# Gated mix of two cached attention branches, one token: the last values in the values' tile, and branch A's output weights in two halves around them

## Chip, cores, metric

The kernel runs on one core of one Trainium2 chip. The metric is device time in microseconds of one execution, the median of several runs.

## What is computed

Two attention branches A and B, each for a batch of 2, one query token, 32 heads of 128 and 4096 cached tokens, all in float32; their outputs are mixed by a gate from the input:

```python
def branch(x, k_cache, v_cache, wq, wo):          # x [2,1,512], caches [2,32,4096,128]
    q = (x @ wq).reshape(B, 1, 32, 128).transpose(0, 2, 1, 3)
    p = softmax(einsum("bhqd,bhkd->bhqk", q, k_cache) * 128 ** -0.5)
    o = einsum("bhqk,bhkd->bhqd", p, v_cache)
    return o.transpose(0, 2, 1, 3).reshape(B, 1, 4096) @ wo     # wo [4096, 512]

x = A_x                                            # both branches take A's input
g = sigmoid((x * gate_w).sum(-1, keepdims=True))
out = g * branch(x, A...) + (1 - g) * branch(x, B...)
```

Nearly all of the data are the four caches, 128 MB each; the four weight matrices have 8 MB each.

## The kernel before

The work is cut into 32 units of 4 heads of one batch entry of one branch. A unit's keys are 8 MB, its values too, and each fills one tile of 128 partitions by 128 tokens by 128 numbers: a partition holds 128 tokens of one head. There are three such tiles, `kt[0]` and `kt[1]` for keys of even and odd units and `vt` for values, and no room for a fourth.

For a unit VectorE (DVE) multiplies the keys by the query (L392), sums over the head's 128 numbers (L395) and finds the maximum (L400 to L402); ScalarE (ACT) takes the exponentials (L367) into `padded` (`pr` in the profile), a tile of weights with empty places that keep heads apart; TensorE (PE) multiplies weights and values in 32 matmuls that add up in PSUM tile `vp` (L371). ACT then clears the used places of `padded` (L430). Units go in pairs, the two batch entries of the same heads. After the second of a pair, `vp` holds both and is picked apart into `vs` (L451, L416).

Each engine runs a loop of its own over pairs (TensorE over units), and semaphores with counts tie them: `k_free[i]` is raised when DVE is done with a keys' tile, `v_free` when ACT has cleared the weights after a unit's products, `summed` when TensorE is done with a unit, `weights` when ACT is, `v_landed` when values have landed. The loads stand on SP's queue, in program order: keys of unit u + 1, values of unit u, each behind a wait for its tile (`load_k`, `load_v`). A wait on SP holds up all requests behind it; the transfers run one behind the other.

The last unit is different. Its values don't go to `vt` but to `kt[0]`, which the last even unit's keys have left, so they can be requested before the product of unit 30 is done. TensorE's loop runs over 31 units (`products(NU - 1)`), and `last_products` multiplies unit 31's values straight from `kt[0]`. Branch A's output weights (`wo["A"]`, one transfer of 8 MB) then go into `vt`, and branch B's into `kt[1]`, in seven transfers that get smaller.

The tail then is: products of unit 31; `vs` of the last pair (L542, L544); per-head sums of `vs` over partitions (L548, `heads`) and of the exponentials (L560, `bank`); division by sums times gate (L575) into `on`; the output product, `project_out` for A's 32 rows and B's first 24 (L466, into `most`), and `project_last` for B's last 8 (L481), which gathers in four PSUM tiles with a folded copy of `most` (L582, L586). The tail's small tiles are cut out of a keys' tile that has been read (`Scratch(kt[0])`).

Of the kernel before, what the change touches and what calls it, by code (L numbers as in the profile page):

```python
# [8 lines left out]
AF = mybir.ActivationFunctionType  # L9
# [4 lines left out]
B = 2  # L14
H = 32
SK = 4096
DH = 128
D = 512
# [3 lines left out]
NS = SK // PH  # L22
# [3 lines left out]
NVC = NS // VC  # L26
QT = 32
STRIPS = P // QT
OR = H * DH // P
# [18 lines left out]
class Streams:  # L48
# [32 lines left out]
    def put(self, e, make, reads=(), writes=(), gives=None):  # L81

        self.before(e, reads, writes)
        i = make(self.engines[e])
        if gives is not None:
            i.then_inc(gives, 1)
            return None
        self.ticks[e] += 1
        i.then_inc(self.sems[e], 1)
        point = self.sems[e], self.ticks[e]  # L90
        self.after(point, reads, writes)
        return point
# [18 lines left out]
class Round:  # L111
# [12 lines left out]
    def do(self, make, after=0, gives=None):  # L124
        self.wait(after)
        i = make(self.x)
        if gives is None:
            self.n += 1
        i.then_inc(gives or self.sem, 1)
        return self.n  # L130
# [13 lines left out]
def tile_gated_decode(ctx: ExitStack, tc: tile.TileContext, ins: dict, out: bass.AP):  # L144
    nc = tc.nc
# [5 lines left out]
    NU = len(units)  # L151
# [5 lines left out]
    slot = small.tile([P, VC], F32, name="slot")  # L157
# [9 lines left out]
    vs = small.tile([P, NP, DH], F32, name="vs")  # L167
# [4 lines left out]
    kt = [big.tile([P, NS, DH], F32, name=f"kt{i}") for i in range(2)]  # L172
    vt = big.tile([P, NS, DH], F32, name="vt")
# [3 lines left out]
    vp = ps.tile([P, VC * DH], F32, name="vp")  # L177
# [4 lines left out]
    with tc.tile_critical(no_gpsimd_drain=True):  # L182
        S = Streams(nc, tc)
        put, take = S.put, S.take
        R = Region
        r_kt = [R(), R()]
        r_vt = R()
        r_pad, r_lp, r_sc, r_across, r_qsel = (R() for _ in range(5))
# [6 lines left out]
        v_landed, k_landed = sem("v_landed"), [sem(f"k_landed{i}") for i in range(2)]  # L195
        v_free, k_free = sem("v_free"), [sem(f"k_free{i}") for i in range(2)]
        weights, summed = sem("weights"), sem("summed")
# [5 lines left out]
        def tokens(cache, u):  # L203
            n, g, b = units[u]
            rows = ins[n + cache].rearrange("b h s d -> (b h s) d")
            r0 = (b * H + g * G) * SK
            return rows[r0:r0 + G * SK].rearrange("(p r) d -> p r d", p=P)
# [3 lines left out]
        def load_parts(item, t, src, slots, *cuts):  # L211
            parts[item] = [S.dma("sp", t[:, i:j], src[:, i:j], slot=s) for s, i, j in zip(slots, cuts, cuts[1:])]

        def arrived(e, item, *which):
            p = parts[item]
            S.wait(e, [p[k] for k in which] if which else p)
# [16 lines left out]
        def load_v(u):  # L233
            if u == 0:
                S.before("sp", [], [r_vt])
            elif u < NU - 1:
                nc.sync.wait_ge(v_free, u)
            if u < NU - 1:
                nc.sync.dma_start(vt, tokens("_v_cache", u)).then_inc(v_landed, 16)
            else:  # L240
                nc.sync.wait_ge(k_free[0], NU // 2)
                load_parts(("v", u), kt[0], tokens("_v_cache", u), "g", 0, NS)

        def load_wo(n):
            t = wo[n]
            src = ins[n + "_wo"].rearrange("(p r) e -> p r e", p=P)
            if n == "A":
                nc.sync.wait_ge(v_free, NU - 1)
                load_parts(("wo", n), t, src, "f", 0, OR)
                return  # L250
            nc.sync.wait_ge(k_free[1], NU // 2)
            load_parts(("wo", n), t, src, "abchi", 0, OR // 2, EARLY, OR - 4, OR - 2, OR - 1)
            parts["wo", n] += [S.dma("sp", t[:, OR - 1, h], src[:, OR - 1, h], slot=s) for s, h in zip("jk", HALVES)]

        wo = {n: t.rearrange("p r d -> p (r d)").rearrange("p (r e) -> p r e", e=D) for n, t in (("A", vt), ("B", kt[1]))}


        class Scratch:
# [3 lines left out]
            def take(self, n):  # L262
                self.at += -(-n // 128) * 128
                return self.t[:, self.at - -(-n // 128) * 128:][:, :n]

        start = Scratch(kt[1]).take
        rows, ident, xg, w, every, e, more = (start(n) for n in (D, P, B * KC, B, P, B, STRIPS * B * G))
        r_rows, r_gatew, r_ident, r_xg, r_w, r_every, r_e, r_more = (R() for _ in range(8))

        def vput(e, make, reads=(), writes=(), **kw):  # L270
# [6 lines left out]
                                     slot="y"))  # L277
# [84 lines left out]
        def exps(u, b, pair, do):  # L362

            s, m = sc[u % 2], nm[u % 2]
            for j, h in enumerate(QUARTERS):
                at = bass.ds(pair * (B * G) + (b * G + j), 1)
                do(lambda x: x.activation(padded[h, :, b, j * VC:(j + 1) * VC], s[h].rearrange("p (c a) -> p c a", a=VC),  # L367
                                          AF.Exp, bias=m[h], accum_out=lp[h, at]), weights if j == G - 1 else None)

        def chunk(x, c, t):  # L370
            return x.matmul(vp[c % STRIPS * QT:(c % STRIPS + 1) * QT], padded[:, c].rearrange("p b m -> p (b m)"),  # L371
                            t[:, c * VC:(c + 1) * VC].rearrange("p a d -> p (a d)"), start=False, stop=False,
                            skip_group_check=True)

        def products(n):
            with nc.Fori(0, n, engines=[mybir.EngineType.PE]):
                take("pe", weights)
                take("pe", v_landed, 16)
                for c in range(NVC):
                    i = chunk(nc.tensor, c, vt)  # L380
                i.then_inc(summed, 1)

        def last_products():
            S.wait("pe", r_pad.writers)
            arrived("pe", ("v", NU - 1))
            for c in range(NVC - 1):
                chunk(nc.tensor, c, kt[0])
            r_kt[0].readers = [put("pe", lambda x: chunk(x, NVC - 1, kt[0]), [], [r_vp])]


        def whole_scores(o, after):
            at = D_.do(lambda x: x.tensor_tensor(kt[o], kt[o], q[:, None, :].to_broadcast([P, NS, DH]), op=ALU.mult), after)  # L392
# [15 lines left out]
        def dve_second(nxt):  # L408
            take("dve", k_landed[1], 16)
            maxima_of(1, whole_scores(1, 0))  # L410
            return next_queries(nxt, 0) if nxt else 0
# [17 lines left out]
        def clear_padded(b):  # L429
            return A_.do(lambda x: x.activation(padded[:, :, b], nil[:, :, None].to_broadcast([P, NVC, G * VC]), AF.Copy))  # L430

        def act_exps(u, b, pair):
            take("act", maxima)
            exps(u, b, pair, lambda make, gives: A_.do(make, 0, gives))

        def act_second(pair, last=False):
            take("act", summed)
            at = clear_padded(0)
            A_.tell(v_free, at)
            A_.tell(spare, at)  # L440
            if not last:
                act_exps(1, 1, pair)
                return
            A_.close()
            take("act", maxima)
            exps(1, 1, pair, lambda make, gives: put("act", make, [], [R()]))
            r_lp.writers = r_pad.writers = [(S.sems["act"], S.ticks["act"])]

        def act_first(pair, nxt):
            take("act", summed)  # L450
# [7 lines left out]


        def project_out(k, n, *rows_):  # L460
            bounds = (0,) if n == "A" else (0, OR // 2)
            for r in range(*rows_):
                if r in bounds:
                    arrived("pe", ("wo", n), bounds.index(r))
                s = r % STRIPS
                put("pe", lambda x: x.matmul(most[s * QT:s * QT + B], on[:, k, r], wo[n][:, r],  # L466
                                             start=n == "A" and r < STRIPS, stop=n == "B" and r >= EARLY - STRIPS),
                    [r_on], [r_most])
# [40 lines left out]
        for u in range(2, NU):  # L509
            load_k(u)  # L510
            load_v(u - 1)
        load_v(NU - 1)
        load_wo("A")
        load_wo("B")

        exps(0, 0, 0, lambda make, gives: put("act", make, [r_nm[0], r_sc, r_pad, r_lp, r_nil], [], gives))
# [6 lines left out]
        with nc.Fori(0, NP - 1, engines=[mybir.EngineType.Activation]) as i:  # L523
            act_second(i)
            act_first(i, i + 1)
        products(NU - 1)
        dve_second(None)
        act_second(NP - 1, last=True)
        D_.close()

        last_products()
        end = Scratch(kt[0]).take
        sums, turned, laid, outs, kept = end(2 * B * P), end(D), end(P), end(P), end(D)
        drawn, onp = end(D), end(2 * OR * B)
        on = onp.rearrange("p (n r b) -> p n r b", n=2, b=B)
        totals = [end(D // 2)[:B] for _ in HALVES]
        r_sums, r_drawn, r_turned, r_laid, r_outs, r_kept = R(), R(), R(), [R() for _ in range(2 * B)], R(), R()
        for r in (r_sums, r_drawn, r_turned, r_outs, r_kept, r_on, *r_laid):
            r.readers = list(r_kt[0].readers)

        last = NP - 1
        put("act", lambda x: x.activation(vs[:, last], vp[:, :DH], AF.Copy, scale=slot[:, :1]), [r_vp], [r_vs])  # L542
        for a in range(1, VC):
            put("dve", lambda x: x.scalar_tensor_tensor(vs[:, last], vp[:, a * DH:(a + 1) * DH], slot[:, a:a + 1], vs[:, last],  # L544
                                                        op0=ALU.mult, op1=ALU.add), [r_vs, r_vp], [r_vs])
# [20 lines left out]
        for n in range(2):  # L566
            for b in range(B):
                c = n * B + b
# [24 lines left out]
        for h, e in enumerate(("sp", "act")):  # L593
            copied, r_total = sem(f"copied{h}"), R()
            for i in range(2):
                _, a, t, _ = next(strips(2 * h + i))
# [28 lines left out]
```

## Time and profile before

| | |
|---|---|
| median of 3 runs | 1324.14 us (1324.11 to 1324.51) |
| profiled execution: span from first to last instruction | 1322.3 us |
| what lies around the span (1324.14 - 1322.3; the profiled execution has no time of its own listed) | 1.8 us |
| moved by DMA | 570.51 MB, 431 GB/s over the span |
| busy: DVE / PE / ACT | 1165.3 / 331.7 / 100.7 us |
| granted TensorE clock, mean | 0.631 |

Times are in microseconds from the span's start unless marked ns. In the profile a line number belongs to the kernel above; a helper's line stands for all that it issues (L106 for the requests of `S.dma`, L97 for the waits of `take`, L134 for the counts of `tell`). `SPq` is SP's queue of requests; `x64` at a matmul counts passes, of which a float32 matmul has two. Requests count as not busy, so the DMA row and the landings show what the transfers do.

### The profile page before, as it was taken

The numbers are of one execution on the slowest core, as the hardware profiler recorded it, in microseconds if no ns is written. First come the engines' busy times: TensorE is split into PE (matmuls) and PEld (weight loads), VectorE is DVE, ScalarE is ACT, GpSimd is POOL, SyncE is SP. The second block draws the span as 40 slices with busy tenths as digits, with TensorE's granted clock in tenths as the row PEclk, the third lists the DMA queues.
The fourth block names the chain that finished last, engine by engine and source line by source line (L and its number), as shares of the span: only waits on it lengthen the run. The fifth ranks groups of instructions, "written<-read, shape, count | busy, mean of one in ns | idle before, by whom it ended". The sixth has DMA issues, their size and how long they took to land. (4 is left out here: it accounts for less than half of the span.)

```text
span 1322.3 us, 6216 instructions
## 1 busy us (share of the span) xinstructions
PE 331.7 (25%) x2382; PEld 90.3 (7%) x2382; DVE 1165.3 (88%) x316; ACT 100.7 (8%) x328; POOL 0.7 (0%) x6
## 2 busy tenths in 40 slices
PE   3112222211222221122222122222212322311256
PEld 0000000000000000000000000000000000000011
DVE  1978999999999999999999999999999999999961
ACT  0000100001010000101000010100001010000100
POOL 0000000000000000000000000000000000000000
PEclk9566666556666655666665666666556666555678
DMA  9999999999999999999999999999999999999998
GB/s 404 453 412 443 442 416 442 442 416 442 442 418 442 440 436 424 442 440 418 442 440 418 442 442 416 442 442 424 436 442 436 422 442 440 418 442 442 417 442 352
DMA packets 10820, 570.51 MB, mean 431 GB/s; under 512 B 1207, under 2 KB 1467, under 8 KB 1726
## 3 DMA queue, kind: packets, MB, share of 16 engines
q1 hardware_dynamic: 10804, 570.43, 99.6%
q8 instruction: 3, 0.05, 0.0%
q14 instruction: 3, 0.02, 0.0%
q10 hardware_dynamic: 10, 0.01, 0.0%
HBM read 570.43 MB, written 0.00 MB: 431 GB/s over the span
## 5 line engine op out<-in xcount | busy, mean ns | idle before, releaser
L392 DVE TENSOR_TENSOR kt<-kt,q 128x16384 f32<-128x16384 f32 x31 | 534.0, 17226 | 71.3 <-DVEq L97 71.3
L395 DVE TENSOR_REDUCE sc<-kt 128x128 f32<-128x16384 f32 x31 | 533.8, 17220 | 1.1
L371 PE MATMUL vp<-vt,pr 128*32 128x512 f32 x1984 | 283.1, 734 | 915.5 <-PEq L97 915.5
L371 PEld LDWEIGHTS vp<-vt,pr 128*32 128x32 f32 x1984 | 77.9, 132 | 1120.7 <-issue 1120.7
L367 ACT ACTIVATE pr<-sc,nm 32x128 f32<-32x128 f32 x128 | 50.9, 398 | 108.1 <-ACTq L97 102.8
L430 ACT ACTIVATE pr<-nil 128x512 f32<-128x512 f32 x31 | 19.3, 623 | 456.8 <-ACTq L97 456.8
L451 ACT ACTIVATE vs<-vp,slot 128x128 f32 x15 | 5.5, 368 | 448.1 <-ACTq L97 448.1
L337 PE MATMUL qa<-vt,cols 128*2 128x512 f32 x128 | 18.4, 739 | 39.9 <-PEq L97 39.9
L367 ACT ACTIVATION_READ_ACCUMULATOR pr<-sc,nm (+1 forms) x128 | 23.5, 184 | 0.0
L416 DVE SCALAR_TENSOR_TENSOR vs<-vp,slot,vs 128x128 f32 x45 | 15.8, 351 | 8.6 <-DVEq L97 7.6
L599 DVE COPY kt<-qa 2x128 f32<-2x128 f32 x1 | 0.3, 278 | 23.8 <-PE qa L481 23.8
L352 DVE STREAM_TRANSPOSE vt<-vt 128x1024 f32<-128x1024 f32 x2 | 2.4, 1224 | 17.1 <-ACT vt L348 17.1
L498 DVE TENSOR_REDUCE sc<-kt 128x64 f32<-128x8192 f32 x2 | 17.4, 8686 | 0.1
L496 DVE TENSOR_TENSOR kt<-kt,q 128x8192 f32<-128x8192 f32 x2 | 17.4, 8688 | 0.0
L455 ACT ACTIVATE vp<-nil 128x512 f32<-128x512 f32 x15 | 9.0, 600 | 99.2 <-ACTq L97 99.2
L544 DVE SCALAR_TENSOR_TENSOR vs<-vp,slot,vs 128x128 f32<-128x128 f32 x3 | 1.1, 351 | 12.9 <-ACT vs L542 12.8
L371 PE MATMUL vp<-kt,pr 128*32 128x512 f32 x64 | 9.0, 724 | 10.9 <-DMA kt<-in_B_v_cache_dram 10.9
L466 PE MATMUL most<-vt,kt 128*2 128x512 f32 x64 | 9.6, 765 | 6.5 <-DMA vt<-in_A_wo_dram 6.5
L400 DVE TENSOR_REDUCE rm<-sc 128x1 f32<-128x128 f32 x31 | 8.7, 281 | 2.3
L406 DVE STREAM_TRANSPOSE q<-qsel 128x128 f32<-128x128 f32 x30 | 9.3, 311 | 1.0
L289 DVE COPY cols<-bank 128x8 f32<-128x8 f32 x1 | 0.2, 167 | 10.0 <-PE bank L287 10.0
L401 DVE STREAM_TRANSPOSE across<-rm 128x32 f32<-128x32 f32 x31 | 6.6, 212 | 1.1
(73 smaller groups left out, 60.4 us busy)
## 6 DMA issues: line engine op xcount, KB each, us to landing
kt<-in_A_k_cache_dram SPq DMA_DIRECT2D x2, 4096.0 KB, 35.6
kt<-in_B_wo_dram SPq DMA_DIRECT2D x1, 4096.0 KB, 33.1
kt<-in_B_wo_dram SPq DMA_DIRECT2D x1, 2048.0 KB, 37.6
kt<-in_B_wo_dram SPq DMA_DIRECT2D x1, 1024.0 KB, 39.5
kt<-in_B_wo_dram SPq DMA_DIRECT2D x1, 512.0 KB, 40.3
vt<-in_A_v_cache_dram SPq DMA_DIRECT2D x16, 28.5
kt<-in_B_k_cache_dram SPq DMA_DIRECT2D x16, 42.6
kt<-in_B_wo_dram SPq DMA_DIRECT2D x1, 256.0 KB, 40.4
```

Of the source, the lines that this page charges most:

```text
L337: last = nc.tensor.matmul(t[h * QT:h * QT + B], cols[:, c], blocks[:, c, i, h], start=c == 0, stop=c == KC - 1)
L367: do(lambda x: x.activation(padded[h, :, b, j * VC:(j + 1) * VC], s[h].rearrange("p (c a) -> p c a", a=VC), AF.Exp, bias=m[h], accum_out=l ...
L371: return x.matmul(vp[c % STRIPS * QT:(c % STRIPS + 1) * QT], padded[:, c].rearrange("p b m -> p (b m)"), t[:, c * VC:(c + 1) * VC].rearran ...
L392: at = D_.do(lambda x: x.tensor_tensor(kt[o], kt[o], q[:, None, :].to_broadcast([P, NS, DH]), op=ALU.mult), after)
L395: at = D_.do(lambda x: x.tensor_reduce(sc[o], kt[o], axis=AX.X, op=ALU.add), at)
L406: return D_.do(lambda x: x.transpose(q, qsel[:, 0].to_broadcast([P, DH // QT, QT])), at)
L416: at = D_.do(lambda x: x.scalar_tensor_tensor(vs[:, g], vp[:, a * DH:(a + 1) * DH], slot[:, a:a + 1], vs[:, g], op0=ALU.mult, op1=ALU.add) ...
L430: return A_.do(lambda x: x.activation(padded[:, :, b], nil[:, :, None].to_broadcast([P, NVC, G * VC]), AF.Copy))
L455: A_.do(lambda x: x.activation(vp, nil.to_broadcast([P, VC * DH]), AF.Copy))
L466: put("pe", lambda x: x.matmul(most[s * QT:s * QT + B], on[:, k, r], wo[n][:, r], start=n == "A" and r < STRIPS, stop=n == "B" and r >= EA ...
L496: put("dve", lambda x: x.tensor_tensor(t, t, q[:, None, :].to_broadcast([P, NS // 2, DH]), op=ALU.mult), [r_q], [r])
L498: put("dve", lambda x: x.tensor_reduce(sc[0][:, h * NS // 2:(h + 1) * NS // 2], t, axis=AX.X, op=ALU.add), [r], [R()])
```

## The change

Unit 31's values go into `vt` like all others, behind a wait for `v_free`, and TensorE's loop runs over all 32 units; `last_products` is gone. Branch A's output weights go into `kt[0]` in two transfers of 4 MB, the first requested ahead of unit 31's values, the second behind them. The tail's small tiles are cut out of `vt`. The wait for the last unit's products is the loop's count `summed`.

```diff
         def load_v(u):
             if u == 0:
                 S.before("sp", [], [r_vt])
-            elif u < NU - 1:
+            else:
                 nc.sync.wait_ge(v_free, u)
-            if u < NU - 1:
-                nc.sync.dma_start(vt, tokens("_v_cache", u)).then_inc(v_landed, 16)
-            else:
-                nc.sync.wait_ge(k_free[0], NU // 2)
-                load_parts(("v", u), kt[0], tokens("_v_cache", u), "g", 0, NS)
+            nc.sync.dma_start(vt, tokens("_v_cache", u)).then_inc(v_landed, 16)
 
-        def load_wo(n):
+        def load_wo(n, h=0):
...
             if n == "A":
-                nc.sync.wait_ge(v_free, NU - 1)
-                load_parts(("wo", n), t, src, "f", 0, OR)
+                if h == 0:
+                    nc.sync.wait_ge(k_free[0], NU // 2)
+                load_parts(("wo", n, h), t, src, "fg"[h], h * OR // 2, (h + 1) * OR // 2)
                 return
...
-        wo = {... (("A", vt), ("B", kt[1]))}
+        wo = {... (("A", kt[0]), ("B", kt[1]))}
...
-        def last_products():
-            S.wait("pe", r_pad.writers)
-            arrived("pe", ("v", NU - 1))
-            for c in range(NVC - 1):
-                chunk(nc.tensor, c, kt[0])
-            r_kt[0].readers = [put("pe", lambda x: chunk(x, NVC - 1, kt[0]), [], [r_vp])]
...
         def project_out(k, n, *rows_):
-            bounds = (0,) if n == "A" else (0, OR // 2)
             for r in range(*rows_):
-                if r in bounds:
-                    arrived("pe", ("wo", n), bounds.index(r))
+                if r % (OR // 2) == 0:
+                    h = r // (OR // 2)
+                    arrived("pe", *((("wo", n, h), 0) if n == "A" else (("wo", n), h)))
...
+        load_wo("A", 0)
         load_v(NU - 1)
-        load_wo("A")
+        load_wo("A", 1)
         load_wo("B")
...
-        products(NU - 1)
+        products(NU)
...
-        last_products()
-        end = Scratch(kt[0]).take
+        end = Scratch(vt).take
...
-        put("act", lambda x: x.activation(vs[:, last], vp[:, :DH], AF.Copy, scale=slot[:, :1]), [r_vp], [r_vs])
+        take("act", summed)
+        r_lp.writers = [put("act", lambda x: x.activation(vs[:, last], vp[:, :DH], AF.Copy, scale=slot[:, :1]), [r_vp], [r_vs])]
```

On SP's queue, at the end of the loads, the requests stand in another order. In these rows `kt_85` is `kt[0]` and `kt_86` is `kt[1]`, and 128x16384 are 8 MB:

```order
 L231 DMA kt_86<-in_B_k_cache_dram 128x16384
-L239 DMA vt<-in_B_v_cache_dram 128x16384
-L106 DMA kt_85<-in_B_v_cache_dram 128x16384
-L106 DMA vt<-in_A_wo_dram 128x16384
+L238 DMA vt<-in_B_v_cache_dram 128x16384
+L106 DMA kt_85<-in_A_wo_dram 128x8192
+L238 DMA vt<-in_B_v_cache_dram 128x16384
+L106 DMA kt_85<-in_A_wo_dram 128x8192
 L106 DMA kt_86<-in_B_wo_dram 128x8192
 L106 DMA kt_86<-in_B_wo_dram 128x4096
```

The last values have moved one place back, behind half of A's weights, and the other half has come behind them.

On TensorE, from the last unit's products to the output rows of branch B, before (with the semaphores that each row waits for; `landed_g` is the last values, `landed_f` A's weights, `landed_a` B's first part):

```order
L371 MATMUL vp<-kt_85,pr 32x512 [waits landed_g,done_act]
L371 MATMUL vp<-kt_85,pr 32x512 x30
L371 MATMUL vp<-kt_85,pr 32x512 [waits done_dve]
L548 MATMUL heads<-vs,pick 32x512 [waits done_dve]
L548 MATMUL heads<-vs,pick 32x512 x3
L560 MATMUL bank<-ones,kt_85 128x1 [waits done_dve]
L560 MATMUL bank<-ones,kt_85 128x1 x3
L466 MATMUL most<-vt,kt_85 2x512 [waits done_dve,landed_f]
L466 MATMUL most<-vt,kt_85 2x512 x31
L466 MATMUL most<-kt_86,kt_85 2x512 [waits landed_a]
```

And the same place after, from the loop that now runs for all 32 units (`landed_f` and `landed_g` are the two halves of A's weights):

```order
L368 MATMUL vp<-vt,pr 32x512 x31
L373 REGISTER_ALU
L373 COMPARE_AND_BRANCH
L535 MATMUL heads<-vs,pick 32x512 [waits done_dve]
L535 MATMUL heads<-vs,pick 32x512 x3
L547 MATMUL bank<-ones,vt 128x1 [waits done_act,done_dve]
L547 MATMUL bank<-ones,vt 128x1 x3
L455 MATMUL most<-kt_85,vt 2x512 [waits done_dve,landed_f]
L455 MATMUL most<-kt_85,vt 2x512 x15
L455 MATMUL most<-kt_85,vt 2x512 [waits landed_g]
L455 MATMUL most<-kt_85,vt 2x512 x15
L455 MATMUL most<-kt_86,vt 2x512 [waits landed_a]
```

The separate 32 products are gone into the loop, and A's output rows wait in two places, at row 0 and at row 16, and no longer once for all.

More of the change, by code (lines that the diff above doesn't have):

```diff
@@ L253, in load_wo @@
             parts["wo", n] += [S.dma("sp", t[:, OR - 1, h], src[:, OR - 1, h], slot=s) for s, h in zip("jk", HALVES)]
-        wo = {n: t.rearrange("p r d -> p (r d)").rearrange("p (r e) -> p r e", e=D) for n, t in (("A", vt), ("B", kt[1]))}
+        wo = {n: t.rearrange("p r d -> p (r d)").rearrange("p (r e) -> p r e", e=D) for n, t in (("A", kt[0]), ("B", kt[1]))}
         class Scratch:
@@ L445, in act_second @@
             take("act", maxima)
-            exps(1, 1, pair, lambda make, gives: put("act", make, [], [R()]))
-            r_lp.writers = r_pad.writers = [(S.sems["act"], S.ticks["act"])]
+            exps(1, 1, pair, lambda make, gives: put("act", make, [], [R()], gives=gives))
         def act_first(pair, nxt):
@@ L537, in tile_gated_decode @@
         r_sums, r_drawn, r_turned, r_laid, r_outs, r_kept = R(), R(), R(), [R() for _ in range(2 * B)], R(), R()
-        for r in (r_sums, r_drawn, r_turned, r_outs, r_kept, r_on, *r_laid):
-            r.readers = list(r_kt[0].readers)
         last = NP - 1
-        put("act", lambda x: x.activation(vs[:, last], vp[:, :DH], AF.Copy, scale=slot[:, :1]), [r_vp], [r_vs])
+        take("act", summed)
+        r_lp.writers = [put("act", lambda x: x.activation(vs[:, last], vp[:, :DH], AF.Copy, scale=slot[:, :1]), [r_vp], [r_vs])]
         for a in range(1, VC):
```

## The prediction, made before the change was run

> **What bounds the kernel now.** I read the page first: shares, queue row, chain.
>
> ```profile
> span 1322.3 us, 6216 instructions
> PE 331.7 (25%) x2382; PEld 90.3 (7%) x2382; DVE 1165.3 (88%) x316; ACT 100.7 (8%) x328; POOL 0.7 (0%) x6
> DMA  9999999999999999999999999999999999999998
> q1 hardware_dynamic: 10804, 570.43, 99.6%
> DMA 3%; DVE 3%; PE 0%; SPq 0%; issue 0%; ACT 0%; DVEq 0%
> DMA kt<-in_B_wo_dram 3%; DVE kt L392 1%; DVE sc L395 1%; PE qa L481 0%; SPq L106 0%; PE vp L481 0%; ACT kt L598 0%; PE qa L586 0%; PE bank L481 0%; DVEq L134 0%; PE bank L586 0%; PE vp L586 0%
> ```
>
> The SP queue's transfers fill 99.6% of the span: the kernel is one stream of 570 MB, and the chain that ends last is its last transfer, branch B's output weights. A change can cost time in two ways: the stream falls dry, or the work behind the last landings outlasts it. Both are decided in the last 90 us, so I went to the timeline there.
>
> ```profile
> 1232.42 0.33 SPq L239 DMA_DIRECT2D vt<-in_B_v_cache_dram  x1
> 1237.55 0.33 SPq L106 DMA_DIRECT2D kt<-in_B_v_cache_dram  x1
> 1241.57 17.23 DVE L392 TENSOR_TENSOR kt<-kt,q 128x16384 f32<-128x16384 f32 x1 [1.40 <-DVEq L97]
> 1260.89 8.42 PE L371 MATMUL vp<-vt,pr 128*32 128x512 f32 x64 [29.66 <-PEq L97]
> 1269.47 0.63 ACT L430 ACTIVATE pr<-nil 128x512 f32<-128x512 f32 x1 [27.49 <-ACTq L97]
> 1270.17 0.33 SPq L106 DMA_DIRECT2D vt<-in_A_wo_dram  x1
> 1276.14 3.44 SPq L106 DMA_DIRECT2D kt<-in_B_wo_dram  x7
> 1280.25 8.98 PE L371 MATMUL vp<-kt,pr 128*32 128x512 f32 x64 [10.94 <-DMA kt<-in_B_v_cache_dram]
> 1289.29 0.37 ACT L542 ACTIVATE vs<-vp,slot 128x128 f32<-128x128 f32 x1 [10.17 <-PE vp L371]
> 1290.94 1.06 PE L548 MATMUL heads<-vs,pick 128*32 128x512 f32 x8 [1.72 <-DVE vs L544]
> 1291.94 1.05 PE L560 MATMUL bank<-ones,kt 128*128 128x1 f32 x8
> 1294.92 0.36 DVE L575 TENSOR_TENSOR kt<-kt,rs 128x64 f32<-128x64 f32 x2
> 1299.47 9.58 PE L466 MATMUL most<-vt,kt 128*2 128x512 f32 x64 [6.49 <-DMA vt<-in_A_wo_dram]
> 1309.28 3.61 PE L466 MATMUL most<-kt,kt 128*2 128x512 f32 x32 [0.23 <-DMA kt<-in_B_wo_dram]
> 1316.57 0.28 PE L481 MATMUL qa<-kt,kt 128*2 128x128 f32 x2 [0.55 <-DMA kt<-in_B_wo_dram]
> 1319.11 0.09 PEld L481 LDWEIGHTS vp<-kt,kt 128*2 128x2 f32 x2 [0.30 <-DMA kt<-in_B_wo_dram]
> 1319.23 0.27 PE L481 MATMUL bank<-kt,kt 128*2 128x128 f32 x1
> ```
>
> Columns: start, duration, engine, line, tile. The starts on landings give the stream's pace: the keys of 1241.57, values of 1260.89 and 1280.25 and A's weights of 1299.47 are 19.32, 19.36 and 19.22 us apart, so 19.3 us per 8 MB and 9.65 per 4 MB. Every request goes out well before the stream reaches it: the last values at 1237.55, when 8 MB queued ahead run until 1260.9; A's weights at 1270.17, 10 us before 1280.25. TensorE waits for a DMA at every step of the tail (6.49 us before A's weights) and ends 0.4 us behind the last landing, at 1319.50.
>
> **The change, part by part.**
>
> *The requests (the main term).* The last values now wait for the values' tile, freed when the product before them is done and ACT has cleared the weights (1269.47 + 0.63): the event that released A's weights at 1270.17. Ahead of them only 4 MB are left, requested at 1237.55; they begin after the values of 1260.89 and are through at 1260.89 + 9.65 = 1270.54. The lead of 10 us shrinks to 0.37 us, less than a request takes to move data. That price is shown where a stream starts empty, at the kernel's start:
>
> ```profile
> 0.96 0.40 SPq L220 DMA_DIRECT2D vt<-in_A_wq_dram  x1
> 23.06 9.49 PE L337 MATMUL qa<-vt,cols 128*2 128x512 f32 x64 [10.68 <-PEq L97]
> vt<-in_A_wq_dram SPq DMA_DIRECT2D x1, 21.8
> 1.80:2.00 0.20, 0.00 (x0) 0.00 (x0) 0.00 (x0) 0.20 (x1) 0.00 (x0) 1.00 1.22 348
> 2.00:2.20 0.20, 0.00 (x0) 0.00 (x0) 0.00 (x0) 0.20 (x1) 0.00 (x0) 1.00 8.86 2949
> ```
>
> The same size into the same tile, into TensorE's loop: 22.10 us from issue to first matmul (21.8 to landing), against 19.3 in a full stream; packets first start about 1.1 us after the issue. So the last values reach TensorE at 1270.17 + 22.10 = 1292.27, not at 1260.89 + 9.65 + 19.3 = 1289.84: a hole of 2.4 us, and everything queued behind (second half of A, all of B) shifts by it. Bounds: 0 if the stream has not drained, 2.4 by this row; I take 2.4, since it is the same request on an empty stream.
> The Trainium skill (DMA: Bandwidth & Descriptors, "Anatomy of one DMA") gives 2.0 us plus bytes at 436 GB/s, an estimate of 21.2 us here against the 21.8 of the row; by it the time would be 0.6 us less. That section is on the other, software-generated path, so I keep the row.
>
> *The clock of TensorE sizes the rest.* The value products do not always take 8.42 us:
>
> ```profile
> 178.94 8.38 PE L371 MATMUL vp<-vt,pr 128*32 128x512 f32 x64 [29.70 <-PEq L97]
> 1145.02 10.03 PE L371 MATMUL vp<-vt,pr 128*32 128x512 f32 x64 [29.79 <-PEq L97]
> L371 PE MATMUL vp<-vt,pr 128*32 128x512 f32 x1984 | 283.1, 734 | 915.5 <-PEq L97 915.5
> ...
> 1280.30:1284.00 3.70, 3.70 (x20) 1.04 (x24) 0.00 (x0) 0.00 (x0) 0.00 (x0) 0.50 1.28 551
> 1284.20:1289.00 4.80, 4.80 (x48) 1.33 (x40) 0.00 (x0) 0.00 (x0) 0.00 (x0) 1.00 1.01 437
> 1293.00:1294.00 1.00, 0.00 (x0) 0.00 (x0) 0.94 (x3) 0.00 (x0) 0.00 (x0) 1.00 0.60 262
> 1295.00:1296.00 1.00, 0.00 (x0) 0.00 (x0) 0.29 (x2) 0.00 (x0) 0.00 (x0) 0.50 2.27 983
> ...
> 1284.75 0.13 PEld L371 LDWEIGHTS vp<-kt,pr 128*32 128x32 f32 x4 [0.30 <-issue]
> 1288.18 0.13 PEld L371 LDWEIGHTS vp<-kt,pr 128*32 128x32 f32 x4 [0.30 <-issue]
> 1316.68 0.28 PE L481 MATMUL qa<-kt,kt 128*2 128x128 f32 x2
> ```
>
> The third column from the right is the granted clock. A run of products starts at 0.50 and is granted 1.00 some 4 us later. At full clock four passes take (1288.18 - 1284.75)/8 = 0.43 us, so 64 passes take 6.86 us and the slow start adds 1.5 to 3.2 us: 8.38 to 10.03, with a mean of 283.1/31 = 9.13 (1984 passes are 31 runs of 64). Which of them a run gets depends on where the clock's own rhythm stands, so I take 9.13 for each of the three such runs on the new path, and keep both ends for the range. After the products the clock fell back between 1293 and 1296, although the head sums (L548, L560) ran until 1292.99. In the new order the output products start 6.1 us after the products end, with only these small matmuls between, so I let them start at half clock too.
>
> *The order of the tail.* A's weights are now half landed before the last values and half 9.65 us behind them, so A no longer waits for a DMA; it waits for the values. What was hidden before is now in a row: products, division and head sums (1289.23 to 1295.28, with the start of the next matmul 6.1 us), A's 32 output rows (64 passes of the products' form), 24 of B's rows (48 passes at full clock, 48 x 0.107 = 5.15 us), and the end: eight rows and the fold, nine steps of two passes, 0.11 us a pass (1316.57 to 1316.68), 2.0 us and 0.15 us of drain. In this execution the division and heads were covered by 6.49 us of waiting for A's weights. That cover is gone.
>
> Sum, on the span's clock:
> - request: 1270.17, moved by the mean run of products in place of the short one of 1260.89 (9.13 - 8.42): 1270.88
> - first product: + 22.10 = 1292.98
> - products + 9.13 = 1302.11; heads and division + 6.1 = 1308.21
> - A + 9.13 = 1317.34; B + 5.15 = 1322.49; end + 2.15 = 1324.64
>
> Against 1319.50 that is 5.1 us later. The last landing, 1319.1 before, moves by 1292.98 - 1289.84 = 3.1 to 1322.2, and B's rows of that part are due after 1324: landings no longer set the end. What follows (two copies, the output's transfer) is unchanged. The span of 1322.3 stands 1.8 us under the median of the runs, 1324.14, which I take as unchanged: 1324.14 + 5.1 = 1329.2.
>
> *At nothing, each with its cover.* One more transfer on SP, 0.33 us: it is issued behind the last values, while the stream has 8 MB to move. B's weights wait for 1276.14 (DVE) as before; SP has passed the values' wait by then. The values' loop has two waits in place of one straight wait: they are inside the 22.10 us, which is also measured into a loop with two. ACT's first copy (L542) waits for the loop's own count, where it waited for TensorE's. The copies of the sums (L556) now wait for ACT too, but stand on DVE behind L544, which does. Each is at most some 0.1 us on the path, either way.
>
> **The rivals.**
> - *TensorE keeps its full clock into the output rows.* Then A takes 6.86 and not 9.13 us: 1322.4, and the last landing (1322.2 plus 0.4) sets the end at 1322.6, 3.1 us late: 1327.2. For it: between L560's end and the first output matmul lie only 2.3 us. Against it: the clock was already at 0.50 in 1295 to 1296, and in the new order those 2.3 us end where it had fallen. The Trainium skill (TensorE: Matmul & The Clock Gate, "HAM oscillation") says that only idle gaps above about 3.4 us cost the clock, which speaks for this rival; the fall here, within 1 to 2 us of the last matmul's end, speaks against the rule, unless such small matmuls do not count as busy. 10%.
> - *The stream does not fall dry* (the other side). If the last values' first packets start before the 16 engines have drained A's half, the products start at 1289.84: 1289.84 + 9.13 + 6.1 + 9.13 + 5.15 + 2.15 = 1321.5, 2.0 us late, 1326.1, which is not to be told from no change. It decides at a hole of about 0.6 us, below which the total stays under the 2.65 us that are 0.2% of the time (about what a measurement of this kernel tells from no change). For it: a lead of 0.37 us; against it: 1.1 us from issue to first packet, and products that take 9.13 in the mean and so leave no lead at all. 8%.
> - *Something makes it faster*, such as a tail that is not reached by the landings I reckon with: all bytes still go through one queue, in the same number, so the last landing can't come earlier. 2%.
>
> **How the numbers follow.** The forecast (hole, and a tail at half clock) has 80%. Its own spread: three runs of products between 8.38 and 10.03 give 2.3 us less to 2.7 us more if all went one way; since they seldom do, about 1.1 each way, and 0.6 less if the start of the stream is cheaper: 1327.5 to 1330.5. To hold 8 in 10 with the rivals I widen it to 1326.4 at the bottom, which takes in the full clock but not the stream without a hole, and to 1331.0 at the top. Slower by over 0.2%: 80% and most of the full clock's case, 87%; within 0.2%: 11%; faster: 2%.
>
> **What would show it.** In the profile after: the request of the last values near 1270 to 1272 with 22 us to landing, where the others have 28 or 43; the products' start near 1292 to 1293.5; GB/s lower for some 2 us near 1271; output rows of A without a wait for a DMA, the first part of them at clock 0.50; and a chain that ends in TensorE and the values' transfer, not in B's weights. The prediction is wrong if the stream shows no hole, if A's rows run at full clock at once, or if TensorE still waits for B's landings at the end.

## The result, and the profile after

The changed kernel takes 1329.98 us, median of 5 runs (1329.71 to 1331.19), against 1324.14 us (1323.96 to 1324.51): 5.8 us slower, ratio 1.0046, interval 1.0035 to 1.0057. The forecast was 1329.2 in a range of 1326.4 to 1331.0. The profiled execution took 1329.71 us, the shortest of the five, with a span of 1327.9. Two executions, one of the kernel before (1378.79 us) and one of the quarter below (1489.03 us), took 4 and 12% longer than the others of their kernels and are left out of the comparisons.

From the page after: the span, the DMA row, the SP queue, and the chain that ended last.

```profile
span 1327.9 us, 6222 instructions
DMA  9999999999999999999999999999999999999997
q1 hardware_dynamic: 10948, 570.43, 99.3%
PE 1%; DVE 0%; ACT 0%; issue 0%
```

The same 570.43 MB now fill 99.3% of a longer span, and the chain has changed hands: before it led through the transfer of branch B's output weights, now it is TensorE's with the steps of DVE and ACT between its matmuls, and no DMA is in it. The timeline of the end (start, duration, engine, line, tiles):

```profile
1260.83 8.82 PE L368 MATMUL vp<-vt,pr 128*32 128x512 f32 x64 [29.26 <-PEq L97]
1269.81 0.63 ACT L420 ACTIVATE pr<-nil 128x512 f32<-128x512 f32 x1 [27.91 <-ACTq L97]
1270.51 0.33 SPq L238 DMA_DIRECT2D vt<-in_B_v_cache_dram  x1
1270.89 0.42 SPq L106 DMA_DIRECT2D kt<-in_A_wo_dram  x1
1276.09 3.72 SPq L106 DMA_DIRECT2D kt<-in_B_wo_dram  x7
1292.79 9.90 PE L368 MATMUL vp<-vt,pr 128*32 128x512 f32 x64 [23.14 <-PEq L97]
1304.43 1.06 PE L535 MATMUL heads<-vs,pick 128*32 128x512 f32 x8 [1.74 <-DVE vs L531]
1305.42 1.05 PE L547 MATMUL bank<-ones,vt 128*128 128x1 f32 x8
1308.91 13.80 PE L455 MATMUL most<-kt,vt 128*2 128x512 f32 x112 [2.44 <-DVE vt L562]
...
1324.52 0.27 PE L470 MATMUL bank<-kt,vt 128*2 128x128 f32 x1
```

The last values are requested at 1270.51, when unit 30's products and ACT's clearing are done. At the stream's pace the 4 MB ahead of them have landed by about 1260.83 + 9.65 = 1270.48, so the lead (the time from a request to the landing of what stands ahead of it) is nothing. The products start at 1292.79, 22.28 us after the request, and all 56 output rows (112 passes) then run without a single wait for a DMA, where TensorE waited 6.49 us for A's weights before. TensorE ends at 1324.79 in place of 1319.50.

The same place in the windows (engines' busy times and counts, then granted TensorE clock, DMA share and GB/s, where a packet counts with all its bytes at its start):

```profile
1268.00:1270.00 2.00, 1.65 (x16) 0.27 (x8) 2.00 (x1) 0.19 (x1) 0.00 (x0) 1.00 0.08 33
1270.00:1271.00 1.00, 0.00 (x0) 0.00 (x0) 1.00 (x1) 0.44 (x1) 0.00 (x0) 1.00 0.00 0
1271.00:1271.50 0.50, 0.00 (x0) 0.00 (x0) 0.50 (x1) 0.00 (x0) 0.00 (x0) 1.00 1.95 655
1271.50:1272.00 0.50, 0.00 (x0) 0.00 (x0) 0.50 (x1) 0.00 (x0) 0.00 (x0) 1.00 4.06 1311
1272.00:1274.00 2.00, 0.00 (x0) 0.00 (x0) 2.00 (x1) 0.00 (x0) 0.00 (x0) 1.00 0.08 33
...
1308.00:1309.00 1.00, 0.09 (x4) 0.12 (x8) 0.70 (x4) 0.00 (x0) 0.00 (x0) 0.89 1.14 492
1309.00:1312.00 3.00, 3.00 (x16) 0.46 (x17) 0.00 (x0) 0.00 (x0) 0.00 (x0) 0.50 0.81 350
1312.00:1316.00 4.00, 4.00 (x40) 0.86 (x36) 0.00 (x0) 0.00 (x0) 0.00 (x0) 0.98 0.98 418
```

Hardly a packet starts between 1268 and 1271, and then all engines start together, as at the kernel's start. By itself that is no hole: hardly one starts between 1272 and 1274 either, while the packets of 1271 to 1272 are under way. The start and duration of each packet in the trace decide it. Before the change 16 packets were under way at every moment from 1262 to 1316. Here 12 of the 16 DMA engines are through with the 4 MB by 1268.7 and the last at 1270.1, and the values' first packets start 0.95 to 1.9 us after the request: on the mean of the engines 2.9 us are empty. So most engines had run dry almost 2 us before the request, and the 4 MB's landing is that of the slowest.

The last three rows show the clock: it falls just as the output rows begin, and half of 1308.9 to 1312 is lost to 0.50.

### The profile page after: what moved, and what is told of

The parts are those of the page before. It is cut to its first block, busy times and chain, and to the rows that moved or that the text cites. A ratio compares the mean times of both kernels' runs of the same rounds, so it can differ in the third digit from the quotient of the medians.

```text
span 1327.9 us, 6222 instructions
## 1 busy us (share of the span) xinstructions
PE 333.1 (25%) x2382; PEld 91.3 (7%) x2382; DVE 1165.1 (88%) x316; ACT 100.7 (8%) x328; POOL 0.7 (0%) x6
## 3 DMA queue, kind: packets, MB, share of 16 engines
q1 hardware_dynamic: 10948, 570.43, 99.3%
HBM read 570.43 MB, written 0.00 MB: 430 GB/s over the span
## 5 line engine op out<-in xcount | busy, mean ns | idle before, releaser
L368 PE MATMUL vp<-vt,pr 128*32 128x512 f32 x2048 | 294.9, 740 | 936.7 <-PEq L97 936.7
L368 PEld LDWEIGHTS vp<-vt,pr 128*32 128x32 f32 x2048 | 81.1, 133 | 1150.5 <-issue 1150.5
L420 ACT ACTIVATE pr<-nil 128x512 f32<-128x512 f32 x31 | 19.3, 623 | 457.6 <-ACTq L97 457.6
L455 PE MATMUL most<-kt,vt 128*2 128x512 f32 x112 | 13.8, 654 | 2.4 <-DVE vt L562 2.4
L334 PEld LDWEIGHTS qa<-vt,cols 128*2 128x2 f32 x128 | 3.5, 99 | 54.3 <-issue 54.3
## 6 DMA issues: line engine op xcount, KB each, us to landing
kt<-in_B_wo_dram SPq DMA_DIRECT2D x1, 2048.0 KB, 40.4
kt<-in_B_wo_dram SPq DMA_DIRECT2D x1, 1024.0 KB, 43.6
```

The costliest lines, as they stand in the source:

```text
L334: last = nc.tensor.matmul(t[h * QT:h * QT + B], cols[:, c], blocks[:, c, i, h], start=c == 0, stop=c == KC - 1)
```

## Experiments

The theory has two terms. The values' request comes too late for the stream (a hole of about 3 us, which shifts everything behind it), and what TensorE does after the values' landing is longer than the transfers that are left, partly at half clock. The rivals: the hole alone is the cost; the clock is not on the path; something else in the change (loop, tile) costs time. Each run was timed beside the kernel before on its chip, whose median was 1323.95 to 1324.06 each time.

### All of A's weights ahead: no hole, and 12 us slower

```diff
...
-                load_parts(("wo", n, h), t, src, "fg"[h], h * OR // 2, (h + 1) * OR // 2)
+                load_parts(("wo", n, h), t, src, "f", 0, OR)
...
-        load_wo("A", 0)
+        load_wo("A")
         load_v(NU - 1)
-        load_wo("A", 1)
```

> All 8 MB of A's output weights are requested ahead of the last values, in one transfer. The stream then has 10 us left when the values' request is made (1270.5), so there is no hole and the last landing is back at 1319.1. Theory (the values' landing plus TensorE's tail sets the end): the products start at 1260.85 + 19.3 + 19.3 = 1299.5, the tail from there to TensorE's end took 32.1 us in the changed kernel, so 1331.6 against 1319.5 before: 1324.1 + 12.1 = 1336.2. Rival (the hole in the stream is the whole cost, the tail is hidden behind B's weights): 1324.1, as before the change.

1335.96 us (1335.87 to 1336.51), ratio 1.0091 (1.0076 to 1.0107). Its timeline:

```profile
1260.87 8.47 PE L367 MATMUL vp<-vt,pr 128*32 128x512 f32 x64 [29.62 <-PEq L97]
1270.19 0.33 SPq L238 DMA_DIRECT2D vt<-in_B_v_cache_dram  x1
1299.53 9.62 PE L367 MATMUL vp<-vt,pr 128*32 128x512 f32 x64 [30.19 <-PEq L97]
1315.36 13.66 PE L454 MATMUL most<-kt,vt 128*2 128x512 f32 x112 [2.44 <-DVE vt L560]
```

The products start 38.66 us after those before them, two full transfers of 19.3: the stream has no hole. Yet the kernel is 6 us slower than with half ahead. So a hole is not needed for the loss: the later place of the values in the stream costs time by itself.

### 20 of 32 rows ahead: most of the hole filled, nothing won

```diff
-                load_parts(("wo", n, h), t, src, "fg"[h], h * OR // 2, (h + 1) * OR // 2)
+                load_parts(("wo", n, h), t, src, "fg"[h], *((0, 20) if h == 0 else (20, OR)))
...
```

> 20 of 32 rows of A's output weights (5.24 MB) are requested ahead of the last values and 12 behind them. The stream then has some 2.8 us left at the values' request, and no hole or nearly none, so the last landing is back at about 1319.1. Theory (values' landing plus tail): the products start at 1260.85 + 12.06 + 19.3 = 1292.2, half a microsecond earlier than with half ahead, so the time hardly moves although the hole is gone: about 1329.3. Rival (the hole is the cost): 1324.2.

1329.63 us (1329.16 to 1330.02), ratio 1.0042 (1.0028 to 1.0056): as with half ahead. Against those before them the products start 1.0 us later than a full stream would have it, so the stream lost a little still:

```profile
1261.03 8.55 PE L368 MATMUL vp<-vt,pr 128*32 128x512 f32 x64 [29.54 <-PEq L97]
1270.44 0.33 SPq L238 DMA_DIRECT2D vt<-in_B_v_cache_dram  x1
1293.42 9.42 PE L368 MATMUL vp<-vt,pr 128*32 128x512 f32 x64 [23.84 <-PEq L97]
```

The last two transfers of B, in the rows of requests (KB each, median us from request to landing), before, in the changed kernel and here:

```profile
kt<-in_B_wo_dram SPq DMA_DIRECT2D x2, 128.0 KB, 39.9
```
```profile
kt<-in_B_wo_dram SPq DMA_DIRECT2D x2, 128.0 KB, 43.9
```
```profile
kt<-in_B_wo_dram SPq DMA_DIRECT2D x2, 128.0 KB, 41.1
```

The stream's end came back by 2.8 of 4.0 us and the time did not follow. With half ahead the end is therefore TensorE's, as its chain says; the values themselves came no earlier (1293.42 against 1292.79).

### None ahead, and a quarter ahead: the stream as the bound

```diff
...
-        load_wo("A", 0)
         load_v(NU - 1)
-        load_wo("A", 1)
+        load_wo("A")
```

> The last values are requested ahead of all of A's output weights: the values in their own tile and in the loop, without any of A's weights to bridge. The request can't go out before 1270.5, so the products start at 1292.8 as with half ahead, and the stream has a hole of 1292.8 - (1260.85 + 19.3) = 12.6 us. Theory and rival agree here: the last landing moves to 1331.7 and ends the kernel, 12.6 us late, 1336.7. It measures the price of a hole by itself. If the time stays near 1330, the stream is not what the requests' order says.

1338.44 us (1337.37 to 1339.16), 14.4 us slower than its kernel before, 1.7 more than expected.

The quarter is the split of the run above with 8 in place of 20.

> 8 of 32 rows of A's output weights (2 MB) are requested ahead of the last values, 24 behind. The values' request goes out at 1270.5 as with half ahead, so the products start at 1292.8 and TensorE's part could end as in the changed kernel; but the hole is 1292.8 - (1260.85 + 4.8 + 19.3) = 7.8 us. Theory: the last landing moves to 1326.9 and now sets the end, 7.8 us late: 1331.9. Rival (only the values' landing counts, the stream behind has room): 1330.0.

1333.76 us (median of 5), 9.8 us slower than its kernel before, 1.9 more than expected.

In both the chain ends in B's weights again, and TensorE waits for them: the stream is the bound when too little bridges the wait. The expected times were too short. In the profiled execution of the quarter 0.6 us of the difference are a longer run of unit 30's products (9.43 us, against 8.82 after the change), so that the request came at 1271.39; and behind a hole B's second part came late by itself. These are the waits of B's first rows in the run with none ahead:

```profile
1321.50 3.62 PE L454 MATMUL most<-kt,vt 128*2 128x512 f32 x32 [0.66 <-DMA kt<-in_B_wo_dram]
1327.38 1.90 PE L454 MATMUL most<-kt,vt 128*2 128x512 f32 x16 [2.27 <-DMA kt<-in_B_wo_dram]
```

The 2 MB of rows 16 to 23 came 5.88 us after the 4 MB of rows 0 to 15; before the change it was 1314.13 - 1309.28 = 4.85. The changed kernel itself has something like it: in the rows of requests B's 2 MB part takes 2.8 us more to land than before (40.4 against 37.6) and the 1 MB part behind it 4.1 us more (43.6 against 39.5). Why the stream loses another 1 us there was not tried, and stays open.

### Without most of A's output rows: the hole by itself

```diff
-        project_out(0, "A", OR)
+        project_out(0, "A", STRIPS)
```

> The changed kernel without 28 of the 32 rows of A's output product (part of the computation is left out), so that TensorE's tail is some 10 us shorter, with all transfers as in the changed kernel. Theory: the tail is then through before the last landing, and what is left is the hole alone, 3.0 us (products start at 1292.79 in place of 1260.83 + 9.65 + 19.3 = 1289.8): 1324.1 + 3.0 = 1327.1, so of the 5.8 us 3.0 are the hole's and 2.8 the tail's. Rival (all of it is the stream): 1330.0, as the changed kernel.

28 of A's 32 output rows are left out, so the output is not the reference's; all transfers stay. 1326.98 us, median of 11 (1326.16 to 1328.08), ratio 1.0021 (1.0012 to 1.0030): 3.0 us over the kernel before, as expected. The profiled execution was the longest, 4.1 us over the kernel before, and its hole was the longer for it: a run of products of 9.87 us put the request off to 1271.81, and the last products started 4.0 us late (1294.04 - 1261.08 - 9.65 - 19.3). With a short tail TensorE waits for B again (in the waits after 1305: engine, tile and line, what it waited for, total, times, longest):

```profile
PE most L455 <- DMA kt<-in_B_wo_dram: 2.4, 1, 2.4
PEld qa L470 <- DMA kt<-in_B_wo_dram: 0.8, 2, 0.6
```

So of the 5.8 us some 3 are what the stream lost, and the rest is TensorE's tail, which outlasts the stream. The two don't add: had the tail been hidden, 3.0 would be left; with most of the hole filled by 20 rows ahead, 1329.63 was left.

### The clock in the tail

Idle matmuls keep TensorE busy in the two gaps of the tail: 7 before the head sums, 10 before the output rows.

```diff
...
+        def keep_busy(m):
+            for _ in range(m):
+                nc.tensor.matmul(spin[:QT], pick, pick[:, None, :].to_broadcast([P, D // QT, QT]), start=True, stop=True)
...
+        keep_busy(7)
         for j in range(STRIPS):
...
+        keep_busy(10)
         project_out(0, "A", OR)
```

> The changed kernel with idle matmuls (pick by itself, into a PSUM bank that nobody reads): 7 between the last products and the head sums, 10 between the sums and the output rows, into gaps of 1.7 and 2.4 us in which TensorE waits. Theory (the output rows start at half clock because the matmuls before them are too few): the rows run at full clock at once, 112 passes in 12.0 us and not 13.8: 1330.0 - 1.8 = 1328.2. Rival (the clock is not on the path, or falls anyway): 1330.0, or later by what the idle matmuls add.

1338.03 us, 14 us over its kernel before and 8 over the changed kernel. The idle matmuls themselves spoiled the experiment. Their group by line (passes | busy, mean ns):

```profile
L375 PE MATMUL spin<-pick 128*32 128x512 f32 x34 | 14.9, 593 | 0.0
```

34 passes took 14.9 us, 0.44 each, four times what the products' passes take. All went to one strip of 32 PSUM partitions; the products go round four strips. They held the output rows back, to 1318.47 from 1308.91. The same mistake made the next run, with idle matmuls after the products of all units but the last too (140 after each, 100 after unit 30), the slowest of all:

```diff
...
-        products(NU)
...
+        products(NU - 2, 140)
+        products(1, 100)
+        products(1)
...
```

> As e5_tail_clock, and after each unit's products idle matmuls too, 140 (30 us) after units 0 to 29 and 100 (21.4 us) after unit 30, so that every run of products finds the clock at full. Theory: products take 7.0 us; the values' request goes out at 1268.6, the products of the last unit start at 1290.8 and end at 1297.9, the output rows end near 1316.1 and TensorE near 1318.3. The tail is then through before the last landing (1319.1 plus a hole of 1.0), and the end is 1.0 us later than before the change: 1325.2. Rival (clock not on the path): 1330 or later.

4048.78 us: 279 of the 280 passes after a unit took 119.9 us, and nothing on the clock's part can be read from it. With `spin[_ % STRIPS * QT:...]`, round the four strips, in the tail alone:

> As e5_tail_clock, but the idle matmuls go round the four strips of PSUM partitions, as the products do, where those of e5 all went to one strip and took 0.43 us a pass in place of 0.11 (20 passes 8.3 us), which pushed the tail itself back. Now 7 of them should take 1.5 us and 10 some 2.1 us, inside gaps of 1.7 and 2.4 us. Theory: the output rows run at full clock at once, 112 passes in 12.0 to 12.2 us and not 13.5 to 13.8: 1330.0 - 1.7 = 1328.3. Rival (the clock falls anyway, or is not on the path): 1330.0 or later.

1328.37 us (1327.53 to 1329.02), ratio 1.0032 (1.0020 to 1.0044). Timeline and windows:

```profile
1302.45 1.90 PE L375 MATMUL spin<-pick 128*32 128x512 f32 x14
1304.37 1.07 PE L543 MATMUL heads<-vs,pick 128*32 128x512 f32 x8
1306.35 2.77 PE L375 MATMUL spin<-pick 128*32 128x512 f32 x20
1308.89 12.24 PE L461 MATMUL most<-kt,vt 128*2 128x512 f32 x112
```
```profile
1309.00:1312.00 3.00, 3.00 (x34) 1.04 (x30) 0.00 (x0) 0.00 (x0) 0.00 (x0) 1.00 0.85 366
```

The output rows start at the same place (1308.89 against 1308.91), at a clock of 1.00 and not 0.50, and take 12.24 us and not 13.80: the fall of the clock in the tail cost 1.6 us in the execution profiled. That is the difference of the two profiled executions too (1328.13 against 1329.71), whose products took nearly the same (9.97 and 9.90). The median is 1.6 us under the 1329.98 of the changed kernel, but the two intervals overlap: the passes in the trace show the clock's part, the medians alone would not. The changed kernel once more, on another chip:

> The changed kernel again, unaltered, on the chip of e10_both, for its spread: 1330.0, between 1329 and 1331.5, as the clock's rhythm falls; e8_tail_strips ran at 1328.4 beside a kernel before at 1324.0.

1329.15 us (1328.78 to 1330.23), ratio 1.0042 (1.0028 to 1.0057): the gain of the held clock in the tail is 0.8 us against this median.

### The clock in every run of products

The run of 4048.78 us again, its idle matmuls round the four strips.

> As e6_all_clock, with the idle matmuls going round the four strips: 140 (30 us) after units 0 to 29, 100 (21.4 us) after unit 30, and those of e8_tail_strips. Theory: every run of products takes 7.0 us; the values' request goes out at 1268.6, the last products start at 1290.8, TensorE is through near 1318.5, before the last landing (1319.1 plus a hole of 1.0): 1324.0 + 1.0 = 1325.0. Rival (the clock is not on the path, or the idle matmuls get in the way): 1330 or later.

1326.26 us, median of 11 (1326.06 to 1326.63), ratio 1.0017 (1.0008 to 1.0026): 2.2 us over its kernel before, where 1.0 was expected.

```profile
1261.12 7.07 PE L369 MATMUL vp<-vt,pr 128*32 128x512 f32 x64 [1.50 <-PEq L97]
1269.04 0.33 SPq L239 DMA_DIRECT2D vt<-in_B_v_cache_dram  x1
1292.41 7.07 PE L369 MATMUL vp<-vt,pr 128*32 128x512 f32 x64 [2.77 <-PEq L97]
1316.50 1.90 PE L461 MATMUL most<-kt,vt 128*2 128x512 f32 x16 [0.23 <-DMA kt<-in_B_wo_dram]
```

Products at full clock take 7.07 us, the request goes out 7.92 us after their start in place of 9.68, and TensorE waits for B's weights again: the tail is hidden, and the hole is left. But the hole did not shrink with the earlier request as expected: the products start 23.37 us after it, and 2.3 us late (1292.41 - 1261.12 - 9.65 - 19.3). By the packets in the trace the engines were empty for 1.0 us on the mean; what makes that 2.3 us at the landing was not followed.

### Both: more ahead, and the clock held

20 of 32 rows ahead, as above, together with the idle matmuls of the last run.

> e2 and e9 together: 20 of 32 rows of A's output weights ahead of the last values, and TensorE's clock held at full in every run of products and in the tail. The values' request goes out near 1269.0 with some 4 us of stream left. Theory (two terms and no third: the hole, and the half clock in a tail that follows the values): the products start at 1261.0 + 12.06 + 19.3 = 1292.4, the tail from there to TensorE's end takes 13.3 + 12.0 + 2.2 = 27.5 us, so 1319.9, and the last landing is back near 1319.3: within 0.5 us of the kernel before, 1324.0 to 1324.5. Rival (something else in the change costs time, such as the loop in place of the straight products, or the other tile): 1325.5 or later.

1326.48 us, median of 11, but spread from 1324.79 to 1327.95; ratio 1.0020 (1.0011 to 1.0029). The profiled execution, of 1324.80 us, was as the theory has it: TensorE through at 1319.89, forecast 1319.9. The median lies where the rival had put it, at 1325.5 or later. A longer execution of the same kernel was profiled too:

> e10_both unaltered, for a second profile: its executions ran from 1324.8 to 1328.0 and the one profiled was among the shortest, with the products starting 23.64 us after their request (1268.61 to 1292.25) and TensorE through at 1319.9. Theory (the rest is in the landing of the last values, since the clock is held): in an execution of 1326.5 or more the products start 1.5 us or more later against the products before them than the 31.57 us of e10_both, or the last landings come later, and the runs of products still take 7.07 us. Rival (the tail on TensorE varies): the products start at the same distance and what follows takes longer.

1326.87 us, median of 8; the profiled execution 1326.91. The two executions, each with the last products and the output rows, and the clock (third from the right) behind their start:

```profile
1292.25 7.07 PE L369 MATMUL vp<-vt,pr 128*32 128x512 f32 x64 [3.03 <-PEq L97]
1305.56 12.25 PE L461 MATMUL most<-kt,vt 128*2 128x512 f32 x112
```
```profile
1292.50:1296.00 3.50, 3.50 (x36) 1.25 (x32) 0.00 (x0) 0.00 (x0) 0.00 (x0) 1.00 1.03 442
```
```profile
1292.41 8.77 PE L370 MATMUL vp<-vt,pr 128*32 128x512 f32 x64 [3.16 <-PEq L98]
1307.42 12.25 PE L462 MATMUL most<-kt,vt 128*2 128x512 f32 x112
```
```profile
1292.50:1296.00 3.50, 3.50 (x20) 1.15 (x23) 0.00 (x0) 0.00 (x0) 0.00 (x0) 0.55 0.99 428
```

My reason for the spread was wrong, and its rival right: the values land at the same distance (31.57 and 31.69 us after the products before them), and the last products take 7.07 us in one and 8.77 in the other. After the idle matmuls TensorE waits 3.0 or 3.2 us for the values, and in one execution the clock outlived that gap and in the other it did not. These 1.7 us are four fifths of the 2.1 between the two times, and the landing's 0.1 is next; the rest was not followed. In both executions no engine ran empty around the request, 4.1 us ahead of the landing (1260.68 + 12.06 - 1268.61 = 4.13), and the products started only 0.2 and 0.3 us later than a full stream would have it. Four of the 19 executions of this kernel stand at 1324.8, among them the first profiled, where the clock held: with both terms taken away the change is 0.85 us over its kernel before (1324.80 against 1323.95). The same loop and the same tile are in it, so they can hardly cost more than that; a kernel with loop and tile alone was not run. None of the versions beats the kernel before.

## Why the prediction was right, step by step

- *The request.* Predicted 1270.88 with a mean run of products (9.13), measured 1270.51 with one of 8.82.
- *The empty stream.* Predicted 22.10 us from request to first product, measured 22.28. The row from the kernel's start, the one other place where the stream is empty, gave the price within 0.2 us. The estimate from the Trainium skill (DMA: Bandwidth & Descriptors, "Anatomy of one DMA", a fit for the software-generated path), 21.2 us to landing, was the poorer: it is 22.1 in the row of requests after the change.
- *The products* took 9.90, predicted 9.13 from a mean; heads and division 6.22 to the next matmul (1302.69 to 1308.91), predicted 6.1.
- *The output rows.* A and B together 13.80 us, predicted 14.28: the half clock at their start was right, and this execution had a short stretch of it (14.71 in the second profile of the changed kernel). The full-clock rival was wrong for the change (0.50 in 1309 to 1312), and right on its size once the clock was held: 12.24 us.
- *The end.* TensorE through at 1324.79, predicted 1324.64; that two errors of 0.8 and 0.5 us went opposite ways is luck as far as these runs tell. The longest of the five, 1331.19, lies above the stated range; the median lies in it. The cover that was lost was smaller than the 6.49 us of the prediction, since TensorE could not have used all of it: the division ended at 1295.28, 4.2 us before A's weights landed. The sum adds up the new path and does not use the 6.49, so it did not suffer.
- *The rival without a hole* fell: the engines were empty for 2.9 us on the mean, and the products came 22 us after the request. The lead that decides was underrated, though. The text put it at about 1.1 us, from request to first packet, and left out that most engines are through well before the landing that it counts from. With a lead of 1.7 us (half ahead and the clock held: 1261.12 + 9.65 - 1269.04) 2.3 us were lost still; with 2.65 us (20 rows ahead: 1261.03 + 12.06 - 1270.44) 1.0 us, which is 1293.42 - 1261.03 - 12.06 - 19.3. With 4.1 us (20 rows and the clock held) 0.2 to 0.3 us were, and with 10 us (all ahead) nothing.
- *The last landing* was predicted at 1322.2; by the rows of requests it moved by 4.0 us (43.9 against 39.9), not 3.1, to about 1323.1. It stayed hidden behind TensorE, so this cost nothing here, but it is the step that would have failed with a shorter tail.

In one sentence: the change moved the values to the place in the stream where their request had no lead, so they came 12.5 us later than before (1292.79 against 1280.25, 9.65 of it for the 4 MB put ahead and 3.0 for the hole), and a tail that had waits for A's and B's weights to hide behind was laid bare.

## To carry to other kernels

In a kernel that one stream of transfers bounds, look for the request with the shortest lead, and price a lost lead by the row of the stream's own start: leads under 3 us were not enough here, and 4.1 us nearly were. Put last in the stream what needs the least work behind it: with the values moved back by 8 MB this kernel lost 12 us although the stream stayed full. And size a short tail on TensorE by the slow passes: the 112 output passes took 12.24 us with the clock held, and 13.55 to 14.71 us in the four profiles where it fell before them.

## What was not expected of the hardware

- Float32 passes of 128x512 took 0.11 us each in turn over four strips of 32 output partitions (112 in 12.24 us) and 0.43 to 0.44 us each on one strip (279 in 119.9 us, 34 in 14.9 us), as if the four strips worked side by side.
- The clock outlived a gap of 3.0 us in one execution and fell around one of 3.2 us in another; in the tail of the changed kernel it fell in a gap of 2.4 us that followed a microsecond of 128x1 matmuls. The Trainium skill (TensorE: Matmul & The Clock Gate, "HAM oscillation") warns of idle gaps above about 3.4 us; these falls came in shorter ones.
- A stream that is nearly empty loses time too: with leads of 1.7 and 2.65 us the values came 2.3 and 1.0 us late, while the engines were empty for 1.0 and 0.5 us on the mean. Part of the rest may be that packets start slowly: the values' first packets of 64 KB, one on each engine, took 2.6 to 3.4 us in the changed kernel, and those of 1274 to 1290 2.4 to 2.7 us. How much it makes was not worked out.
